# A mixer kernel on one core: the loads of w_v issued by GpSimd instead of SP

## The chip, the cores and the metric

The kernel runs on one core of a Trainium2 chip. The metric is the device time of one execution in microseconds (us); a row of times is the median of several executions. Besides the executions that are only timed, one is recorded by the hardware profiler, and all rows below are from that one.

## What is computed

Three stages follow each other; the batch is 4, the sequence 576 long, the model 512 wide with 8 heads of 64.

```python
# 1. causal attention with a bias from cumulative sums of s, 32 (batch, head) pairs
scores = scale * q @ k.T + min(-(cum_i - cum_j), 0);  attn = softmax(scores);  x = attn @ v
# 2. channel mix, d_ff = 1024
xk = mu_k * x + (1 - mu_k) * x_prev;  xr = mu_r * x + (1 - mu_r) * x_prev
k = relu(xk @ w_k);  v = (k * k) @ w_v;  r = sigmoid(xr @ w_r);  x = r * v
# 3. token mix (576 -> 256 -> 576) and channel mix (512 -> 1536 -> 512), both with a residual
u = x + token_mix(x);  out = u + relu(u @ w_ch1) @ w_ch2
```

The weights arrive with 8 bytes per element. So w_v, which is 1024 x 512, is 4 MB in memory, and each element has to be put together from two 32-bit words before TensorE can use it.

## The kernel before

The program is written as ordinary Python loops, and each piece of work carries a place in an order (`at(place)`). A planner then goes through all pieces, takes for each engine the one with the lowest place among those that are ready, and fixes one list per engine; the chip runs these five lists, each strictly in order, with semaphores between them. A DMA stands in the list of the engine that issues it. It holds that list for the time of its issue and, if what it writes into is still in use, until that is released. What stands behind it on that engine waits too.

The attention of batch 0 comes first. `early` (L301) does the first two blocks of 128 queries of its 8 heads, `late` (L350) the other three. They run scores on TensorE (L308, L358), a masked maximum on VectorE (L252), the exponential on ScalarE (L262), the sum's reciprocal on VectorE (L263, L264), the normalization of P on GpSimd (L265), transposes on TensorE (L316, L367), a copy on ScalarE and the product with v on TensorE (L326, L385). In the meantime the weights of stage 2 are prepared. Then come the attention of batches 1 to 3 (L277, L399, L447) and beside it the matmuls of stage 2: `up` with w_k (tile h), `gate` with w_r (tile r), `down` with w_v (tile vd), all at L109. Stage 3 ends the program, with nearly nothing but matmuls.

A weight is prepared piece by piece. `weight_load` (L538) takes a buffer and issues the load (L543) on the queue that its last argument names, SP if there is none. `weight_split` (L551) puts the two words together and splits the result into a high and a low part: two ScalarE instructions (L75, L555), two on VectorE (L556, L557), for w_v a halving on ScalarE, a copy of the high part on ScalarE (L75), and the subtraction that gives the low part (L561). That last one is on VectorE for w_v and on GpSimd for the other weights. It is also what releases the buffer. w_k and w_r come in 12 pieces of 512 KB, through five buffers of their own. w_v comes in 16 pieces of 256 KB. These pieces take their buffers from the pool `xt`, which has 6 and which also holds the attention's results `xt`, four of them for batch 0 from L329 on. That leaves two for the pieces of w_v. The weights of stage 3 (w_tok1, w_tok2, w_ch1, w_ch2) come much later, from the function `weight`, in 58 pieces of 128 to 288 KB; their loads are issued by GpSimd.

SP issues everything else: the loads of q, k and v, copies inside the chip (X<-HL, X<-ext_d), the stores.

The pieces of w_v have places from 18 on, in steps of 1.5; the first `late` item has place 16, the pieces of w_k and w_r have places 1.0 to 14.2.

```python
    x = 18
    for f in range(0, DM, 128):
        for k in range(0, KF, 2):
            with at(x):
                weight_load((k, f), rows(w_v, k, k + 2)[:, :, f:f + 128], S // 2, xt_p, "xt")
                weight_split((k, f), wv[:, 0, k:k + 2, f:f + 128], wv[:, 1, k:k + 2, f:f + 128], 1)
            x += 1.5
```

Of the kernel before, what the change touches and what calls it, by code (L numbers as in the profile page):

```python
# [24 lines left out]
def attention_moe_mixer(  # L25
# [16 lines left out]
    nc = tc.nc  # L42
    G, D, _, S = qk.shape
# [24 lines left out]
    def at(place):  # L68
        return tc.high_priority(tc.cur_priority - int(place * 1000))
# [13 lines left out]
    xt_p = ctx.enter_context(tc.tile_pool(name="xt", bufs=6))  # L83
# [60 lines left out]
    xt = {}  # L144
# [394 lines left out]
    def weight_load(key, sw, n, pool, tag, q=nc.sync):  # L539
        r, k, f = sw.shape  # L540
        t = pool.tile([128, n, 2], I32, tag=tag, name="raw")[:, 0:k * f].rearrange("p (k f) t -> p k f t", f=f)
        for r0 in range(0, 128, r):
            q.dma_start(out=t[r0:r0 + r], in_=sw.bitcast(I32).rearrange("p k (f t) -> p k f t", t=2))  # L543
        raw[key] = t
# [6 lines left out]
    def weight_split(key, hi, lo, half=0):  # L551
        t = raw.pop(key)
        low, high = t[:, :, :, 0], t[:, :, :, 1]
        copy("A", f32(high), f32(high), 2.0 ** -112)
        nc.scalar.activation(out=low.bitcast(U32), in_=low.bitcast(U32), func=AF.Copy, scale=TOP3, bias=-0.496)  # L555
        nc.vector.scalar_tensor_tensor(out=low, in0=high, scalar=3, in1=low, op0=ALU.logical_shift_left, op1=ALU.bitwise_or)  # L556
        nc.vector.scalar_tensor_tensor(out=low, in0=high, scalar=-2 ** 31, in1=low, op0=ALU.bitwise_and, op1=ALU.bitwise_or)  # L557
        if half:
            copy("A", f32(low), f32(low), 0.5)
        copy("A", hi, f32(low))  # L560
        (nc.vector if half else nc.gpsimd).tensor_tensor(out=lo, in0=f32(low), in1=f32(hi), op=ALU.subtract)  # L561

    def rows(sw, k0, k1):
        r0 = 128 * k0
        r = min(128, sw.shape[0] - r0)
        return sw[r0:r0 + r * (k1 - k0)].rearrange("(k p) f -> p k f", p=r)
# [119 lines left out]
    for y, a in enumerate(first):  # L686
        nm, W, sw, f = a
# [15 lines left out]
    for f in range(0, DM, 128):  # L703
        for k in range(0, KF, 2):
            with at(x):
                weight_load((k, f), rows(w_v, k, k + 2)[:, :, f:f + 128], S // 2, xt_p, "xt")
                weight_split((k, f), wv[:, 0, k:k + 2, f:f + 128], wv[:, 1, k:k + 2, f:f + 128], 1)
            x += 1.5
    with at(N0):
# [228 lines left out]
```

## Time and profile before

| | |
|---|---|
| median of 3 executions | 905.09 us (903.65 to 905.67) |
| profiled execution, its own time | 905.17 us |
| its span, first to last instruction | 903.4 us |
| TensorE matmul busy | 861.6 us (95%) |
| VectorE, ScalarE, GpSimd busy | 515.1, 464.8, 318.5 us |
| mean granted TensorE clock | 0.977 |

The profiled execution lies 0.08 us from the median, so its rows stand for the timed executions. 1.77 us of its time lie outside the span. PE is TensorE's matmuls, PEld its weight loads, DVE VectorE, ACT ScalarE, POOL GpSimd, SPq the DMA issues of SP. L543 is line 543 of the program. An arrow `<-` in brackets names what ended an idle time; `X<-HL` names a tile and what it is made from.

### The profile page before, as it was taken

To read this page: it belongs to the slowest core of one execution; us is meant where nothing else is said; L and a number is where in the kernel's file an instruction comes from. 1 tells how busy PE (TensorE), PEld (TensorE's weight loads), DVE (VectorE), ACT (ScalarE), POOL (GpSimd) and SP (SyncE) were. 2 spreads that over 40 slices of the span, in tenths; PEclk is the share of its full clock that TensorE was granted. 3 is DMA by queue.
4 is the path that set the end of the run, shared out by engine and by line. 5 is a ranking of instruction groups with operands and counts; after the bars stand their busy time and mean duration, and the time that the engine had idled before them with its cause. 6 is when DMAs were issued, how large, how long until landed. Compare 5 with 4: busy or idle time off the path is not lost.

```text
span 903.4 us, 16007 instructions
## 1 busy us (share of the span) xinstructions
PE 861.6 (95%) x5456; PEld 789.6 (87%) x5456; DVE 515.1 (57%) x1542; ACT 464.8 (51%) x1264; POOL 318.5 (35%) x463
## 2 busy tenths in 40 slices
PE   6679999999899999999999998999999999999998
PEld 4335678998789989989989998999999999999998
DVE  5687786777898587876657865871331212212120
ACT  4787876766786756758456774760320201112010
POOL 4555535644564535655144764550000000000000
PEclk9759999999999999999999999999999999999999
DMA  7973345456654336542032656564022020211100
GB/s 168 215 193 89 88 124 133 98 122 152 139 117 107 88 81 142 121 108 48 29 118 78 216 160 200 183 180 129 24 75 66 18 79 27 63 43 53 36 1 36
DMA packets 65089, 93.69 MB, mean 104 GB/s; under 512 B 7424, under 2 KB 45568, under 8 KB 65008
## 3 DMA queue, kind: packets, MB, share of 16 engines
q1 hardware_dynamic: 58560, 77.00, 33.1%
q0 software_dynamic: 4576, 15.08, 5.5%
q10 hardware_dynamic: 1872, 0.59, 0.3%
q8 instruction: 43, 0.70, 0.3%
q14 instruction: 38, 0.31, 0.1%
HBM read 56.11 MB, written 14.75 MB: 78 GB/s over the span
## 4 chain that ended last, share of the span: by engine, by line
PE 77%; DMA 8%; DVE 7%; ACT 3%; issue 2%; POOL 2%; SPq 0%; ACTq 0%; POOLq 0%; DVEq 0%
PE c L109 33%; PE vd L109 9%; PE h L109 9%; PE r L109 5%; PE t L109 5%; PE pv L447 4%; PE t L399 3%; PE s L358 3%; PE s L277 2%; PE pv L385 2%; PE s L278 2%; DMA X<-HL 2%; DMA raw<-in_moe_w_k_dram 1%; PE t L367 1%; DVE raw L556 1%
## 5 line engine op out<-in xcount | busy, mean ns | idle before, releaser
L784 ACT ACTIVATE HID<-c 128x384 fp32r<-128x384 f32 x72 | 35.4, 491 | 220.6 <-PE c L109 220.5
L265 POOL TENSOR_SCALAR P<-P,sum 64x576 f32<-64x576 f32 (+4 forms) x160 | 106.5, 670 | 113.9 <-DVE sum L264 58.5
L109 PE MATMUL h<-XK,WK 128*128 128x256 f32 (+1 forms) x768 | 122.9, 301 | 3.6 <-DVE XK L465 1.5
L109 PE MATMUL vd<-KK,WV 128*128 128x256 f32 (+1 forms) x768 | 119.3, 299 | 0.0
L109 PEld LDWEIGHTS h<-XK,WK 128*128 128x128 f32 x768 | 105.6, 188 | 7.9 <-DVE XK L465 2.1
L262 ACT ACTIVATE P<-P,mx 64x576 f32<-64x576 f32 (+4 forms) x160 | 95.8, 600 | 30.7 <-DVE mx L252 26.7
L109 PEld LDWEIGHTS vd<-KK,WV 128*128 128x128 f32 x768 | 105.8, 188 | 2.2 <-ACT raw L555 0.4
L109 PE MATMUL c<-HID,WV 128*128 128x384 f32 x576 | 104.9, 336 | 0.0
L109 PE MATMUL c<-U,WK 128*128 128x384 f32 x576 | 104.2, 337 | 0.5 <-DVE HID L785 0.5
L109 PEld LDWEIGHTS c<-U,WK 128*128 128x128 f32 x576 | 99.9, 188 | 1.1 <-DVE HID L785 0.8
L109 PEld LDWEIGHTS c<-HID,WV 128*128 128x128 f32 x576 | 100.7, 188 | 0.0
L252 DVE CUSTOM_DVE_ANT_0 P<-s,maskc 64x288 f32<-64x288 f32 (+4 forms) x160 | 75.0, 474 | 26.3 <-PE t L399 6.9
L785 DVE SCALAR_TENSOR_TENSOR HID<-c,HID 128x384 fp32r<-128x384 f32 x72 | 40.0, 556 | 87.0 <-ACT HID L784 86.9
L842 DVE TENSOR_TENSOR ut<-c,ut 128x384 f32<-128x384 f32 x24 | 13.4, 558 | 124.1 <-PE c L109 124.1
L477 POOL TENSOR_TENSOR KK<-k,KK 128x256 fp32r<-128x256 f32 (+1 forms) x64 | 54.1, 848 | 31.5 <-ACT k L476 31.2
L109 PE MATMUL r<-XR,WR 128*128 128x320 f32 (+1 forms) x384 | 60.0, 298 | 0.0
L556 DVE SCALAR_TENSOR_TENSOR raw<-raw 128x256 int32<-128x256 int32 (+2 forms) x85 | 47.1, 556 | 19.6 <-ACT raw L555 15.7
L75 ACT ACTIVATE raw<-raw 128x256 f32<-128x256 f32 (+2 forms) x101 | 46.9, 465 | 19.6 <-DMA raw<-in_moe_w_v_dram 6.6
L399 PE MATMUL t<-ident,P 128*128 128x128 f32 (+1 forms) x360 | 53.6, 262 | 2.1 <-DVE PT L425 1.6
L109 PE MATMUL c<-HID,WR 128*128 128x384 f32 x288 | 54.2, 336 | 0.0
L109 PEld LDWEIGHTS r<-XR,WR 128*128 128x128 f32 x384 | 53.0, 188 | 0.7
L109 PE MATMUL c<-U,C1A 128*128 128x384 f32 x288 | 52.9, 343 | 0.0
(111 smaller groups left out, 1627.6 us busy)
## 6 DMA issues: line engine op xcount, KB each, us to landing
X<-HL SPq DMA_DIRECT2D x72, 288.0 KB
raw<-in_moe_w_ch_dram POOLq DMA_DIRECT2D x48, 256.0 KB, 3.3
HL<-in_qk_dram SPq DMA_DIRECT2D x12, 576.0 KB
ut<-u_d SPq DMA_DIRECT2D x32, 192.0 KB
yt<-y_d SPq DMA_DIRECT2D x16, 288.0 KB
u_d<-yt SPq DMA_DIRECT2D x16, 288.0 KB
raw<-in_moe_w_k_dram SPq DMA_DIRECT2D x8, 512.0 KB
raw<-in_moe_w_v_dram SPq DMA_DIRECT2D x16, 256.0 KB
```

What stands on the lines that cost most here:

```text
L75: nc.scalar.activation(out=out, in_=in_, func=AF.Copy, scale=scale)
L109: nc.tensor.matmul(ps, a, b, start=first and i == 0, stop=last and i == n - 1)
L252: nc.vector.tensor_tensor_reduce(out=P[0:m, c0:c1], in0=ps[0:m, 0:c1 - c0], in1=maskc[0:m, 512 - q0 + c0:512 - q0 + c1], scale=-scale, sca ...
L262: nc.scalar.activation(out=P[0:m, 0:w], in_=P[0:m, 0:w], func=AF.Exp, bias=mx[0:m, x:x + 1], scale=-1.0, accum_out=sm[0:m, 0:1])
L265: nc.gpsimd.tensor_scalar(out=P[0:m, 0:w], in0=P[0:m, 0:w], scalar1=sm[0:m, 1:2], scalar2=1.0, op0=ALU.mult, op1=ALU.mult)
L358: nc.tensor.matmul(ps[0:m, 0:c1 - c0], x[0:D + 4, 0, q0:q0 + m], x[0:D + 4, 1, c0:c1], start=True, stop=True)
L399: nc.tensor.transpose(ps[0:r, p0 + m * k:p0 + m * k + m], P[0:m, 128 * k:128 * k + r], ident[0:m, 0:m])
L447: nc.tensor.matmul(ps[:, o:n], vv[0:r, k, :], pair[t], start=(k == 0 and t == 0), stop=(k == nk - 1 and t == 1),)
L477: nc.gpsimd.tensor_tensor(out=kk[:, 1, m, 0:n], in0=t[:, 0:n], in1=f32(kk[:, 0, m, 0:n]), op=ALU.subtract)
L556: nc.vector.scalar_tensor_tensor(out=low, in0=high, scalar=3, in1=low, op0=ALU.logical_shift_left, op1=ALU.bitwise_or)
L784: nc.scalar.activation(out=hi, in_=ps, func=AF.Relu)
L785: nc.vector.scalar_tensor_tensor(out=lo, in0=ps, scalar=0.0, in1=f32(hi), op0=ALU.max, op1=ALU.subtract)
```

## The change

The call that loads a piece of w_v is given a queue, GpSimd's. Pieces, sizes, buffers, places and the split stay as they are.

```diff
     for f in range(0, DM, 128):
         for k in range(0, KF, 2):
             with at(x):
-                weight_load((k, f), rows(w_v, k, k + 2)[:, :, f:f + 128], S // 2, xt_p, "xt")
+                weight_load((k, f), rows(w_v, k, k + 2)[:, :, f:f + 128], S // 2, xt_p, "xt", nc.gpsimd)
                 weight_split((k, f), wv[:, 0, k:k + 2, f:f + 128], wv[:, 1, k:k + 2, f:f + 128], 1)
             x += 1.5
```

## Rows read from the trace of the kernel before

**Rows 1.** The page's parts on the span and the engines' busy time.

```profile
span 903.4 us, 16007 instructions
PE 861.6 (95%) x5456; PEld 789.6 (87%) x5456; DVE 515.1 (57%) x1542; ACT 464.8 (51%) x1264; POOL 318.5 (35%) x463
```

**Rows 2.** Table by stretch: busy us of each engine, granted clock, DMA share, GB/s.

```profile
0.00:10.00 10.00, 3.24 (x10) 2.53 (x10) 4.88 (x22) 2.33 (x5) 3.67 (x21) 1.00 0.55 98
10.00:40.00 30.00, 21.44 (x70) 12.62 (x68) 18.84 (x78) 20.30 (x54) 14.72 (x26) 0.90 0.96 211
40.00:52.00 12.00, 11.30 (x21) 4.82 (x21) 7.43 (x20) 8.74 (x22) 7.74 (x9) 0.50 0.99 304
52.00:67.00 15.00, 10.23 (x29) 4.50 (x29) 14.60 (x37) 12.90 (x30) 7.26 (x5) 0.61 0.60 137
67.00:80.00 13.00, 11.07 (x57) 6.21 (x56) 8.83 (x27) 8.40 (x24) 8.14 (x8) 0.96 0.34 88
80.00:140.00 60.00, 60.00 (x386) 44.37 (x385) 45.42 (x148) 46.48 (x138) 26.23 (x36) 1.00 0.40 106
140.00:600.00 460.00, 444.53 (x3138) 416.28 (x3137) 342.96 (x1074) 318.19 (x893) 247.68 (x358) 0.99 0.47 122
```

**Rows 3.** Timelines around 63 to 73 us (start, duration): PE, POOL, then DVE.

```profile
72.39 0.51 PE L367 MATMUL t<-ident,P 64*128 64x64 f32 x5 [1.93 <-POOL P L265]
...
63.12 2.94 POOL L265 TENSOR_SCALAR P<-P,sum 128x384 f32<-128x384 f32 x1 [3.79 <-DVE sum L264]
...
88.18 0.59 POOL L265 TENSOR_SCALAR P<-P,sum 128x384 f32<-128x384 f32 x1 [1.08 <-ACT k L476]
...
62.85 0.40 DVE L556 SCALAR_TENSOR_TENSOR raw<-raw 128x256 int32<-128x256 int32 x1
...
64.61 0.41 DVE L557 SCALAR_TENSOR_TENSOR raw<-raw 128x256 int32<-128x256 int32 x1
...
65.61 1.32 DVE L557 SCALAR_TENSOR_TENSOR raw<-raw 128x256 int32<-128x256 int32 x2
```

**Rows 4.** Loads of w_v on SP: all 16 together, then two rows of SP's timeline.

```profile
L543 SPq DMA_DIRECT2D raw<-in_moe_w_v_dram x16: 367/370/1398, 38.6 to 123.9; - x16
...
38.62 1.64 SPq L543 DMA_DIRECT2D raw<-in_moe_w_v_dram  x2
...
70.33 0.37 SPq L543 DMA_DIRECT2D raw<-in_moe_w_v_dram  x1
```

**Rows 5.** Waits (us in total, times, longest): SP's and TensorE's weight loads'.

```profile
SPq L543 <- DVE WV L561: 20.3, 4, 13.6
...
PEld vd L109 <- DVE WV L561: 0.4, 1, 0.4
```

**Rows 6.** Line 543, 390 to 610 us: GpSimd's loads (ns min/median/max), their waits, their landing.

```profile
L543 POOL DMA_DIRECT2D raw<-in_moe_w_ch_dram x48: 536/546/633, 489.6 to 597.0; - x48
L543 POOL DMA_DIRECT2D raw<-in_moe_w_tok_dram x10: 530/550/732, 393.5 to 486.3; - x10
...
  DVE t L463: 3.4, 2
  DVE U L830: 2.8, 2
  DVE sum L263: 2.2, 1
...
DMA to landing us min/median/max: 2.4/3.3/5.5
```

**Rows 7.** Timelines of the opening: GpSimd's, then TensorE's first matmuls.

```profile
2.73 0.21 POOL L329 MEMSET xt<- 128x1 f32 x4
...
3.22 0.38 POOL masks.py:199 TENSOR_SCALAR_AFFINE_SELECT ident<-ident 128x128 f32<-128x128 f32 x1
9.35 0.95 POOL L185 MEMSET e<- 32x192 f32 x4 [5.76 <-DMA ext_d<-e]
...
6.76 1.62 PE L308 MATMUL s<-HL 66*128 66x128 f32 x4 [6.76 <-DMA HL<-in_qk_dram]
```

## The prediction

> **What bounds the kernel now.** I read the page's busy times first. TensorE's matmuls are busy for 861.6 of the 903.4 us of the span, GpSimd for 318.5 [rows 1]. So the first question is where TensorE is not busy. The table by stretch answers it [rows 2]. From 80 to 140 us TensorE is busy for all 60 us, and after that for 444.5 of 460 us until 600. The loose part is the opening: 3.2 of the first 10 us, 21.4 of the next 30, 10.2 of the 15 us from 52 on, 11.1 of the 13 from 67 on. Whatever brings the start of the full stretch forward is worth its whole length at the end, since the matmuls behind it are the same; whatever happens beside the full stretch is worth nothing unless TensorE comes to wait for it.
>
> In the opening the limit changes. [...] From 52 to 67 us VectorE is full, 14.6 of 15 us [rows 2]. Then GpSimd is last: at 72.39 us TensorE's transposes had waited 1.93 us for a normalization of P on GpSimd, and the one that began at 63.12 us took 2.94 us where the same shape took 0.59 us at 88.18 us [rows 3].
>
> The loads of w_v stand in this picture as follows. SP issues 16 of them, the first two at 38.62 us, the last at 123.9 us [rows 4]. Two buffers carry all 16, so from the third on a load waits for the subtraction L561 of the piece two before it. SP's list was held up by that for 20.3 us in 4 waits, once for 13.6 us, which ends with the load at 70.33 us [rows 4, 5]. TensorE has no large wait from these pieces: its weight loads for vd waited 0.4 us for w_v's last step [rows 5].
>
> **The change, part by part.** *Removed from SP:* 16 issues of 0.37 us (the median; the longest is 1.40 us), 5.9 us of issuing, and the 20.3 us of waits that stood in front of SP's later loads and stores [rows 4, 5]. I cost the gain at nothing. In the full stretch TensorE waits for none of SP's transfers, and the load that was held for 13.6 us had behind it only loads for later heads. If that cover is gone, SP's transfers are at most earlier.
>
> *Added to GpSimd:* 16 issues. The 58 loads that GpSimd issues later in the program show the price: 0.53 to 0.73 us each, median 0.55 us, so 8.7 us in all [rows 6]. In the full stretch of 60 us GpSimd is busy for 26.2 us, so the 33.8 us of idle time take in some 12 of them, 6.6 us, at no cost. From 67 to 80 us GpSimd is on the path. There two loads fall now (one at 70.33 us [rows 4], the next close behind). On the path both would cost 1.1 us, behind the normalizations none. I take one, +0.55 us.
>
> *Added waits:* a load in GpSimd's list waits there for its buffer, and behind it stand the normalizations of P (TensorE's transposes wait for them) and the subtractions for w_r. Of the 58 later loads, 5 waited for VectorE, 8.4 us in all, 1.7 us each [rows 6]. The planner puts a load behind what it takes to be done by the time of the release, so I take 0 here and put the wait among the rivals.
>
> *Moved in time:* GpSimd has nothing to do from 3.6 us, where the last step for the identity ends, until 9.35 us. The four memsets of `xt` at 2.73 us, which belong to heads 1, 3, 5 and 7, show that its list takes whatever is ready, out of the program's order [rows 7]. At that time the two spare buffers are free. So I expect the first two loads of w_v in this gap and not at 38.62 us. That has two consequences. The first is on the DMA engines. 0.52 MB leave the stretch from 40 to 52 us, where 304 GB/s were moved at a share of 0.99: a gain of up to 1.7 us. They come into the first 10 us, where the share is 0.55, so some 4.5 us of the engines' time are free; at the 211 GB/s of the next stretch the two loads want 2.5 us [rows 2]. They fit, but they share the engines with the first loads of q and k, for which TensorE waits until 6.76 us [rows 7]; that could cost up to 2.5 us. I take half of the gain, -0.8 us, as TensorE at half clock is a limit of that stretch as well.
>
> The second consequence is on VectorE. With the first pieces split early, the third and fourth get their buffers early as well. Their four instructions (first at 62.85, last within 65.61 us, three of 0.4 us and a part of 1.32 us, some 1.9 us) leave the stretch in which VectorE is full and in which GpSimd's 2.94 us normalization lies [rows 2, 3]. That normalization is 2.35 us over its price elsewhere, which bounds the gain; the other bound is 0, if the fifth and sixth piece take the same place. I take the four instructions' own time, -1.9 us.
>
> [...]
>
> *At the end of w_v:* pieces that run one round ahead take away the 0.4 us that vd's weight loads waited [rows 5], -0.4 us.
>
> **The sum.** +0.55 - 0.8 - 1.9 - 0.4 = -2.55 us, against the profiled execution's 905.17 us (span 903.4 and 1.77 around it): 902.6 us. That execution lies 0.08 us from the median of the runs, so no correction is made. With all gains at their bounds and no issue on the path it is -2.35 - 1.7 - 0.4 = -4.45 us, 900.7 us.
>
> **The rivals.** *No change.* What bounds the opening is work that the change doesn't touch (VectorE's instructions on w_k and w_r, the attention), and the fifth and sixth pieces take the place of the third and fourth; the full stretch hides the rest. For it speaks that TensorE waits for w_v only 0.4 us [rows 5]. Then all terms but small ones are 0, and the time is 905.2 us. [...]
>
> *GpSimd held by a load.* Slower: a load in the stretch from 67 to 80 us reaches the head of GpSimd's list before its buffer is free, and a normalization of P that TensorE is waiting for stands behind it. It decides from the point where the subtraction that releases the buffer comes later on VectorE than the planner took it to. For it: one such wait on SP lasted 13.6 us [rows 5], and GpSimd is the last releaser just there [rows 3]. Against it: 53 of 58 later loads did not wait [rows 6]. Two loads at 0.55 + 1.7 us are +4.5 us with no gain: 909.7 us.
>
> *The early loads crowd the opening.* The 2.5 us bound above falls on the path of q and k and of the first piece of w_k, and no gain follows: 907.7 us. For it speaks that the DMA engines are full from 10 us on [rows 2], against it the idle 4.5 us before.
>
> *Late landing.* The loads from GpSimd land in 5.5 us, the longest of the later ones, not in 3.3 us, the median [rows 6]. Through two buffers that adds 2.2 us in each of 7 rounds, 15.4 us for the last piece; less a lead of about a round (some 11 us: the loads run from 38.6 to 123.9 us in 8 rounds) it is some +4 us: 909 us. [...]
>
> **How the numbers follow.** The forecast has a chance of 0.40, no change 0.27, GpSimd held 0.18, the crowded opening 0.11, late landing 0.04. About 0.2%, 1.8 us, is what a measurement of this kernel can tell from no change. So faster is 0.40, the same 0.27, slower 0.33. The range runs over the rivals on the slow side to 909.7 us; on the other side it starts at 900.7 us. The planner lays all five lists anew, and TensorE idles for 15.5 us between 140 and 600 us [rows 2], which a new order can move either way. I add a sixth of that, some 2.5 us, at each end: 898 to 912 us.
>
> **What would show it.** Right: two loads of w_v on GpSimd before 10 us; the second pair well before 48 us; no 2.9 us normalization near 63 us; the full stretch of TensorE beginning 2 to 3 us earlier than about 72.4 us, with the same busy time behind it. Wrong: the first loads still near 38 us (then no change), an idle time of GpSimd in front of L543 of over 1 us followed by TensorE's transposes waiting (held), TensorE's first matmul clearly after 6.76 us (crowded). A different order of stage 2 between 140 and 600 us, with TensorE's idle time moved by several us there, would make the prediction wrong for a reason that no row of before shows.

## The result, and the profile after

The changed kernel takes 909.94 us, median of 7 runs (906.87 to 912.39), beside 905.09 us for the kernel before in the same rounds: ratio 1.0053, 95% interval 1.0033 to 1.0073. It is slower by about 4.8 us, where 2.5 us less were forecast. The profiled execution took 911.34 us, 6.2 more than that of before. Some of the shortened kernels below ran in two groups of executions 1 to 3% apart; where a median has a second one beside it, that one is of the faster group.

The page of the kernel after, its parts on the span and on TensorE's busy time (beside [rows 1]):

```profile
span 909.4 us, 16008 instructions
PE 867.7 (95%) x5456; PEld 793.1 (87%) x5456; DVE 520.9 (57%) x1542; ACT 461.3 (51%) x1264; POOL 325.9 (36%) x479
```

The 16 loads are there (479 instructions on GpSimd for 463). The table by stretch of the kernel after, with the columns of [rows 2]:

```profile
0.00:10.00 10.00, 1.81 (x6) 1.67 (x7) 4.47 (x16) 2.66 (x6) 5.54 (x23) 1.00 0.70 150
10.00:40.00 30.00, 23.82 (x67) 13.62 (x65) 22.52 (x93) 25.85 (x73) 19.10 (x29) 1.00 1.06 278
40.00:52.00 12.00, 11.37 (x24) 4.87 (x25) 10.05 (x24) 7.67 (x17) 7.84 (x11) 1.00 0.91 238
52.00:67.00 15.00, 9.11 (x25) 4.27 (x24) 14.97 (x30) 10.91 (x27) 6.63 (x7) 1.00 0.25 75
67.00:80.00 13.00, 12.86 (x54) 6.88 (x54) 8.68 (x32) 8.55 (x25) 8.14 (x9) 1.00 0.24 68
80.00:140.00 60.00, 59.62 (x377) 43.10 (x378) 45.02 (x140) 41.89 (x122) 27.53 (x41) 1.00 0.37 98
140.00:600.00 460.00, 443.25 (x3119) 414.46 (x3118) 338.69 (x1064) 312.48 (x885) 244.40 (x354) 0.99 0.47 120
```

Three things are to be seen. The DMA engines now work in the first 40 us (278 GB/s for 211) and have little to do from 52 us on. From 52 to 67 us VectorE is full still, 14.97 of 15 us, but with 30 instructions where it did 37. And TensorE got less far: 25 matmuls from 52 to 67 us for 29, 54 from 67 to 80 us for 57, and 377 from 80 to 140 us for 386. Busy time alone would have said the contrary for 67 to 80 us.

The 1.00 in the clock column up to 67 us must not be read as full speed. The trace of the kernel after has no reading of the clock before 73.3 us (that of before none before 27 us), and the column then shows 1.00. Matmuls of one shape tell more. In the kernel before, two products `s` of 68x288 at a reading of 1.00, two of 68x512 at 0.50, and the clock there (TensorE's busy time, matmuls, clock, DMA share, GB/s):

```profile
54.48 0.70 PE L358 MATMUL s<-X 68*64 68x288 f32 x2
61.70 2.07 PE L358 MATMUL s<-X 68*128 68x512 f32 x2 [2.90 <-DVE mx L252]
54.50:57.50 3.00, 1.14 (x5) 1.00 1.04 191
60.00:65.00 5.00, 3.30 (x5) 0.50 0.13 41
```

and in the kernel after:

```profile
66.02 2.08 PE L358 MATMUL s<-X 68*128 68x512 f32 x2 [0.73 <-DVE mx L252]
```

The two of 68x288 take 1.22 us there (at 60.80 us, below). By these times TensorE at 61 and 66 us after still ran as it does at a reading of 0.50, as it mostly did from 34 to 68 us before (0.50 from 34 to 52 us, 0.61 in the mean from 52 to 67 us).

GpSimd's loads of w_v in the kernel after (ns min/median/max, idle time before them, who waited, landing), beside [rows 4 to 6]:

```profile
L543 POOL DMA_DIRECT2D raw<-in_moe_w_v_dram x16: 722/758/879, 2.9 to 114.1; - x16
its engine sat idle before it (us, times) until:
  DVE WV L561: 12.4, 7
  DVE sum L263: 6.8, 2
  DVE t L462: 0.6, 1
who waited for it (us, times):
  ACT raw L75: 11.0, 7
...
DMA to landing us min/median/max: 3.0/4.0/7.5
```

An issue takes 0.76 us, not 0.55; ten of the 16 had to wait, 19.8 us in all. And their places, from GpSimd's timeline of the kernel after (the first six):

```profile
2.89 1.62 POOL L543 DMA_DIRECT2D raw<-in_moe_w_v_dram  x2
...
13.29 0.74 POOL L543 DMA_DIRECT2D raw<-in_moe_w_v_dram  x1 [2.80 <-DVE sum L263]
...
16.13 0.76 POOL L543 DMA_DIRECT2D raw<-in_moe_w_v_dram  x1
...
27.30 0.76 POOL L543 DMA_DIRECT2D raw<-in_moe_w_v_dram  x1 [4.94 <-DVE WV L561]
...
39.12 0.76 POOL L543 DMA_DIRECT2D raw<-in_moe_w_v_dram  x1
```

When the kernel before issues its first, the kernel after issues its sixth. That pulls the split of w_v forward, into the time in which w_k and w_r are split and the attention starts. The work on the tile `raw` (all pieces of w_k, w_r and w_v) by stretch, after and then before (columns: VectorE, ScalarE, GpSimd with instructions, clock, DMA share, GB/s):

```profile
0.00:40.00 40.00, 13.59 (x24) 17.39 (x36) 11.64 (x11) 1.00 0.97 246
40.00:67.00 27.00, 18.64 (x18) 13.72 (x27) 7.55 (x6) 1.00 0.54 147
```

```profile
0.00:40.00 40.00, 9.59 (x12) 10.95 (x18) 6.02 (x4) 0.92 0.86 183
40.00:67.00 27.00, 13.65 (x22) 15.44 (x32) 6.16 (x5) 0.56 0.77 211
```

VectorE has done 42 such instructions by 67 us, in 32.2 us; in before 34, in 23.2 us. That is 9 us more of the engine that limits the stretch, for eight more instructions. One row explains nearly half of it. VectorE's timeline of the kernel after:

```profile
55.22 0.40 DVE L556 SCALAR_TENSOR_TENSOR raw<-raw 128x256 int32<-128x256 int32 x1
55.65 4.62 DVE L557 SCALAR_TENSOR_TENSOR raw<-raw 128x256 int32<-128x256 int32 x1
60.19 0.55 DVE L252 CUSTOM_DVE_ANT_0 P<-s,maskc 128x384 f32<-128x384 f32 x1
60.66 0.08 DVE L252 DVE_READ_ACCUMULATOR2_ANT mx<- 128x1 f32 x1
```

and GpSimd's at the same time:

```profile
50.72 0.76 POOL L543 DMA_DIRECT2D raw<-in_moe_w_v_dram  x1 [0.57 <-DVE WV L561]
51.53 0.72 POOL L265 TENSOR_SCALAR P<-P,sum 128x512 f32<-128x512 f32 x1
52.23 1.73 POOL L561 TENSOR_TENSOR WK<-raw,WK 128x512 fp32r<-128x512 f32 x1
55.47 0.76 POOL L265 TENSOR_SCALAR P<-P,sum 64x576 f32<-64x576 f32 x1 [1.51 <-DVE sum L264]
56.20 1.29 POOL L561 TENSOR_TENSOR WK<-raw,WK 128x512 fp32r<-128x512 f32 x1
57.46 2.52 POOL L561 TENSOR_TENSOR WR<-raw,WR 128x512 fp32r<-128x512 f32 x2
```

The bitwise operation of 0.41 us [rows 3] took 4.62 us. It began as GpSimd was in the first of four instructions that follow each other without a gap, and ended 0.3 us after the last. The same instruction takes 4.62 us in e6, a further run with all loads on GpSimd. Behind it stands the step on P of shape 128x384 that TensorE waits for: TensorE's next product `s` had waited 3.65 us, as its timeline in the kernel after shows:

```profile
60.80 1.22 PE L358 MATMUL s<-X 68*64 68x288 f32 x2 [3.65 <-DVE mx L252]
```

GpSimd's four took 0.76, 1.29 and, two together, 2.52 us, and VectorE's instruction did not end between any two of them. What in the hardware holds it these rows do not show.

To see where the lag arises I compare at equal matrix work: the matmuls are summed in order, each with the median distance from one of its shape to the next in the trace of before, and the times are compared at which the same sum is reached. In us later than before, at the time of before in the first line (the rows e1, e3 and e16 are runs told of below):

```
                          20    57    88   195   246   289   374   end
after                    2.0   6.1   1.8   1.3   1.8   3.9   6.1   6.0
e1  first two           -1.0   2.4   0.8   0.8   4.7   5.4   4.9   7.0
e16 3rd to 8th on SP    -1.0  -2.1  -3.4  -3.4   0.7   5.3   4.2   4.2
e3  SP, other order     -1.9  -0.6  -0.6  -0.2   1.3   1.1   2.0  -0.5
```

After is 6 us behind at 57 us and makes up for most of it, since TensorE is not full before 80 us; 1.8 us stay at 88 us. The rest of the 6.0 us comes later: the lag is 3.9 us at 289 us, some 2 us again at 364 us, and 6.1 us at 374 us, far behind the last piece of w_v. There TensorE's timeline of the kernel after has

```profile
372.21 1.57 PE L447 MATMUL pv<-PT,VV 128*128 128x320 f32 x8 [1.82 <-DVE xt L454]
```

and its table the stretch

```profile
370.00:377.00 7.00, 5.18 (x28) 4.73 (x26) 6.72 (x25) 6.31 (x21) 6.38 (x9) 0.76 0.65 129
```

with 28 matmuls in 7 us, at a mean clock of 0.76 behind a gap; the same stretch in the kernel before has 58 at full clock:

```profile
370.00:377.00 7.00, 7.00 (x58) 6.53 (x57) 5.87 (x21) 6.93 (x22) 7.00 (x11) 1.00 0.57 129
```

There are two questions, then: what the loads cost in the opening, and what a new order of the instructions costs behind it.

### The profile page after: what moved, and what is told of

Same layout as the page of the kernel before. It is cut to its first block, busy times and chain, and to the rows that moved or that the text cites. A ratio compares the mean times of both kernels' runs of the same rounds, so it can differ in the third digit from the quotient of the medians.

```text
span 909.4 us, 16008 instructions
## 1 busy us (share of the span) xinstructions
PE 867.7 (95%) x5456; PEld 793.1 (87%) x5456; DVE 520.9 (57%) x1542; ACT 461.3 (51%) x1264; POOL 325.9 (36%) x479
## 4 chain that ended last, share of the span: by engine, by line
PE 71%; DMA 10%; DVE 9%; issue 5%; ACT 3%; POOL 2%; SPq 1%; POOLq 0%; ACTq 0%; DVEq 0%
PE c L109 32%; PE vd L109 8%; PE h L109 7%; PE r L109 5%; PE t L109 4%; PE pv L447 3%; PE t L399 3%; DMA X<-HL 3%; PE s L277 2%; DMA HL<-in_qk_dram 2%; PE s L278 2%; PE pv L385 1%; DVE raw L556 1%; DMA raw<-in_moe_w_k_dram 1%; DVE P L252 1%
## 5 line engine op out<-in xcount | busy, mean ns | idle before, releaser
L265 POOL TENSOR_SCALAR P<-P,sum 64x576 f32<-64x576 f32 (+4 forms) x160 | 101.6, 640 | 114.9 <-DVE sum L264 45.1
L109 PE MATMUL h<-XK,WK 128*128 128x256 f32 (+1 forms) x768 | 125.0, 304 | 1.9 <-ACT k L474 1.1
L109 PEld LDWEIGHTS h<-XK,WK 128*128 128x128 f32 x768 | 108.5, 192 | 5.3 <-ACT k L474 1.5
L556 DVE SCALAR_TENSOR_TENSOR raw<-raw 128x256 int32<-128x256 int32 (+2 forms) x85 | 44.9, 529 | 24.1 <-ACT raw L555 20.5
L557 DVE SCALAR_TENSOR_TENSOR raw<-raw 128x256 int32<-128x256 int32 (+2 forms) x85 | 57.3, 678 | 1.1
```

Of the source, the lines that this page charges most:

```text
L109: nc.tensor.matmul(ps, a, b, start=first and i == 0, stop=last and i == n - 1)
L265: nc.gpsimd.tensor_scalar(out=P[0:m, 0:w], in0=P[0:m, 0:w], scalar1=sm[0:m, 1:2], scalar2=1.0, op0=ALU.mult, op1=ALU.mult)
```

## The experiments

**Parts of the change in the whole kernel.** The loads are divided between the two issuers:

```diff
-weight_load((k, f), ..., S // 2, xt_p, "xt", nc.gpsimd)
+weight_load((k, f), ..., S // 2, xt_p, "xt", nc.gpsimd if f == 0 and k < 4 else nc.sync)   # e1: first two
+weight_load((k, f), ..., S // 2, xt_p, "xt", nc.sync if f == 0 and k < 4 else nc.gpsimd)   # e2: last 14
```

> Only the first two pieces of w_v are loaded from GpSimd, the other 14 from SP as before. Theory A (the pieces now come too early: the first two loads at 3 us share the DMA engines with q and k, and their successors bring VectorE work into 40 to 67 us): TensorE's full stretch begins about 2 us late as in the changed kernel, and the time is 1 to 3 us over before, apart from what a new order later does. Theory B (GpSimd's list is held by issues and waits of the 16 loads): 14 of the 16 holds are gone, the opening is as before within 0.5 us. Theory C (the planner's new order of stage 2 and of batches 1 to 3 makes the difference): the time can be anywhere within 4 us of before, and the lag at the start of stage 3 isn't the one at 85 us.

Measured 910.49 us (904.78 to 913.22), ratio 1.0040 [1.0010, 1.0070].

> The first two pieces of w_v stay on SP and so are loaded near 38 us, the other 14 are loaded from GpSimd. Theory A: no load of w_v before 38 us, so the opening is as before within 0.5 us, and the time too, apart from a new order later. Theory B: 14 issues of 0.76 us and their waits for buffers stay in GpSimd's list; TensorE is 1 to 2 us late by 135 us. Theory C: anywhere within 4 us of before, decided after 200 us.

Measured 916.31 us (914.64 to 923.03), ratio 1.0137 [1.0070, 1.0204]. Each part alone is as bad as the whole or worse, so the time is no sum of the parts. By the table at equal work, e1 is 0.8 us behind at 195 us and 4.7 at 246 us. Whatever costs it most lies where w_v has long been loaded. It doesn't strike each time: of e1's ten executions three took 904.8 to 905.6 us, as long as before, and seven 910.2 to 913.2.

**Another order behind the opening, with the loads left where they are.** The units of stage 2 get another place in the planner's order; the lists are the same up to about 120 us and are planned anew behind it:

```diff
-            with at(N0 + n + 3):
+            with at(N0 + n + 3.3):   # e3 (loads on SP), e4 (on GpSimd); 2.7 for e11 (SP), e12 (GpSimd)
```

> The kernel before with one number changed that has nothing to do with loads: the units of stage 2 get a place 0.3 later. The lists of all engines stay the same up to about 120 us and are planned anew after it. Theory C: the time moves by 2 to 6 us from before in either direction. Theories A and B: by under 1.5 us.

> The changed kernel with the same number changed as in the run before it (the units of stage 2 a place 0.3 later). Theory C: the difference to its partner with SP is not 5 us but the 1 to 2.5 us that the opening has, or even has the other sign, as the orders after 120 us are new for both. Theories A and B: again some 5 us slower than its partner.

> The whole kernel before with the units of stage 2 a place 0.3 earlier: the same opening, another order behind 120 us than that of before and than the one with places 0.3 later. Theory C (a new order by itself costs some us, because that of before happens to be a good one): 3 to 6 us over before. Otherwise within 1.5 us of it, as with the places 0.3 later (0.7 us over).

> The whole changed kernel with the units of stage 2 a place 0.3 earlier. If the cost is the opening's 3.1 us alone, 3 us over its partner with SP; if the loads on GpSimd cost something behind the opening as well, 5 to 9 us, as in the two pairs so far (4.9 and 8.9 us).

Measured, beside the two kernels themselves:

```
place      loads on SP              loads on GpSimd          distance
+3         905.09                   909.94                    4.8
+3.3  e3   906.83 (904.70-912.03)   e4  915.70 (910.63-918.66)  8.9
+2.7  e11  916.13 (908.20-918.72)   e12 913.27 (909.23-915.30) -2.9
```

The same loads with another order behind them differ by up to 11 us on SP (905.1 to 916.1) and 5.8 on GpSimd. The distance of the pairs is 3.6 us in the mean, with both signs, though the negative one is not sure: e11's five executions alone span 908 to 919 us. A single pair of whole kernels therefore can't tell what the loads cost. The part up to where the lists are the same can. At equal work, at 88 us, the three openings with the loads on GpSimd (after, e4, e12) are 1.8, 2.7 and 1.7 us behind before, and the two others with SP (e3, e11) 0.6 and 2.9 us ahead of it. So executions of the same opening differ by up to 2.9 us, and the two kinds by 3.2 us in the mean, without overlap.

**The opening by itself.** Batches 1 to 3, the second half of stage 2 of batch 0 and stage 3 are left out; the results so far are stored. What remains has the lists of the whole kernels up to 95 to 125 us:

```diff
-    for n in range(NI):
+    for n in range(N1):
         attention_item(n)
...
+            nc.sync.dma_start(out=out[0, 128 * p:128 * p + 128, :], in_=xt[0, p][:, 1:1 + S])
```

> The kernel before, cut: it leaves out batches 1 to 3 of the attention, the second half of batch 0 of stage 2 and all of stage 3, and stores the attention's result of batch 0. The lists are those of before up to about 125 us. It is the yardstick for the three runs beside it; about 145 to 155 us.

> The changed kernel, cut in the same way, so that the opening is measured by itself and nothing that is planned anew behind it counts. If the loss sits in the opening (theories A and B), it is 2 to 4 us slower than its yardstick with SP; if it comes from the new order behind it (theory C), within 0.7 us of it.

> The same cut with only the first two loads of w_v on GpSimd, the other 14 on SP. Theory A (too early): as slow as with all 16, 2 to 4 us over the yardstick. Theory B (GpSimd's list held): within 0.7 us of the yardstick.

> The same cut with the first two loads on SP and the last 14 on GpSimd. Theory A: within 0.7 us of the yardstick. Theory B: 2 to 4 us over it.

Two more divide the loads at the eighth (`nc.gpsimd if f < 256 else nc.sync`, and the reverse):

> The cut of before's opening again (batches 1 to 3, the second half of batch 0 of stage 2 and stage 3 left out), with the first 8 loads of w_v on GpSimd and the last 8 on SP. The yardstick with SP took 147.6 us, all 16 on GpSimd 150.7, the first two alone 145.4. If the cost comes from loads 3 to 8, which hold GpSimd's list before TensorE's full stretch, 150 to 151 us; if it comes from the loads in the full stretch from 80 us on, 145 to 146 us.

> The same cut with the first 8 loads on SP and the last 8, all of them in or just ahead of TensorE's full stretch, on GpSimd. If the full stretch hides GpSimd's issues and waits, 147.6 us within 0.7; if they count there too, 149 us or more.

Measured, and the distance to e5 (all executions, then the faster group):

```
e5   all on SP                  147.61 (146.52-150.38)          147.09
e6   all on GpSimd              150.69 (150.08-153.19)   +3.1   150.62   +3.5
e7   first two on GpSimd        145.42 (144.69-147.06)   -2.2   145.42   -1.7
e8   last 14 on GpSimd          149.57 (148.97-150.57)   +2.0   149.57   +2.5
e9   first eight on GpSimd      153.75 (152.27-155.75)   +6.1   152.59   +5.5
e10  last eight on GpSimd       147.69 (146.84-151.50)   +0.1   147.65   +0.6
```

Here the change costs 3.1 us, or 3.5. The first two loads gain some 2 us, and the last eight, which fall beside the full stretch, cost 0.1 to 0.6. What costs comes with the third to eighth: e9 less e7 is 8.3 us (7.2 in the faster group), e8 less e10 is 1.9 us. The size depends on the company, the sign doesn't.

Not all of this is time that GpSimd or VectorE takes. From 70 to 80 us, where TensorE's first matmuls with w_k fall, its rows in e5, e8 and e10 are (columns as above):

```profile
70.00:80.00 10.00, 8.31 (x47) 1.00 0.55 144
70.00:80.00 10.00, 9.92 (x30) 0.66 0.33 85
70.00:80.00 10.00, 10.00 (x24) 0.51 0.31 87
```

At equal work e8 was 2.4 us ahead of before at 65 us and 1.5 behind at 80 us; e10 went from 2.7 ahead to 3.6 behind, and e5 stayed 0.7 ahead. The lists of e5 and e10 are the same up to 92 us, and the profiled execution of e10 is its longest, 151.50 us, where the other four took 146.84 to 147.79. So executions of the same lists that differ in the clock lie 4.3 us apart at 80 us, and e8 was no later than e5 until its clock fell. How far the distances in the table come by way of the clock was not taken apart.

**Is GpSimd's bunch the cause?** Without w_r's low half two of the four instructions beside the 4.62 us are gone, while VectorE's list stays the same to beyond the step on P:

```diff
-        (nc.vector if half else nc.gpsimd).tensor_tensor(out=lo, in0=f32(low), in1=f32(hi), op=ALU.subtract)
+        lo is None or (nc.vector if half else nc.gpsimd).tensor_tensor(out=lo, in0=f32(low), in1=f32(hi), op=ALU.subtract)
...
-weight_split((nm, f), W[:, 0, :, f:f + 128], W[:, 1, :, f:f + 128])
+weight_split((nm, f), W[:, 0, :, f:f + 128], W[:, 1, :, f:f + 128] if W is wk else None)
```

> All 16 loads of w_v on GpSimd, shortened opening, and GpSimd's four subtractions that make the low half of w_r left out (the product with w_r reads the high half twice instead), so that two of the four GpSimd instructions that ran back to back at 55.5 to 60.0 us are gone (WR x2, 2.52 us). The lists of VectorE are the same to the normalization multiply behind it. Theory H (the loads hold GpSimd, its instructions bunch up behind, and VectorE's bitwise operation on `raw` 128x256 is held for the whole bunch, 4.62 us against 0.41): that instruction falls to about 2.0 us, `P` 128x384 on VectorE comes at about 57.7 us instead of 60.4, and the time lies 2 to 3 us under the 150.7 of the same opening with the subtractions. Theory V (it is w_v's split work that stands earlier in VectorE's and ScalarE's lists, whatever GpSimd does): the time falls by no more than that of the opening with SP's loads when it loses the same four instructions, and the pair stays 3 us apart.

> The control: loads on SP, shortened opening, the same four subtractions left out and the high half read twice. Both theories: 147.6 less 0 to 1 us, since in that opening no VectorE instruction is held longer than about 1.8 us.

VectorE's timeline of e13:

```profile
54.77 2.13 DVE L557 SCALAR_TENSOR_TENSOR raw<-raw 128x256 int32<-128x256 int32 x1
56.82 0.55 DVE L252 CUSTOM_DVE_ANT_0 P<-s,maskc 128x384 f32<-128x384 f32 x1
```

and GpSimd's of e13:

```profile
54.59 0.77 POOL L265 TENSOR_SCALAR P<-P,sum 64x576 f32<-64x576 f32 x1 [1.51 <-DVE sum L264]
55.33 1.29 POOL L561 TENSOR_TENSOR WK<-raw,WK 128x512 fp32r<-128x512 f32 x1
```

The instruction falls from 4.62 to 2.13 us and again ends 0.3 us behind GpSimd's last, as theory H has it, and the whole falls by 2.6 us to 148.07 (147.91 to 148.74). That the bunch holds VectorE is thus shown. But the control e14 fell by 5.2 us, to 142.44 (140.15 to 144.01; faster group 140.67), where 0 to 1 was expected, so the distance of the pair grew to 5.6 us. By the totals that is what theory V was to give. The lists of each are those of its original up to about 65 us, so equal work compares them where before stands at 57 us: there GpSimd's opening lies 6.7 us behind SP's with the subtractions and 2.7 us without. So the bunch makes some 4.0 of 6.7 us at that point, as far as single traces can tell: two of the same lists lie up to 2.9 us apart. The rest is something else: in VectorE's timeline of e14 the same step on P stands at

```profile
52.44 0.55 DVE L252 CUSTOM_DVE_ANT_0 P<-s,maskc 128x384 f32<-128x384 f32 x1
```

4.4 us before e13's, of which the held instruction explains 1.7 (2.13 less 0.41). In VectorE's list 16 of the second bitwise operations stand ahead of that step with the loads on GpSimd, nine with SP. What the new lists behind 65 us contribute to e14's end was not taken apart.

**Does it add up, and is there a better division?** Loads 3 to 8 go back to SP, the others stay on GpSimd, in the opening (e15) and in the whole kernel (e16):

```diff
+weight_load((k, f), ..., S // 2, xt_p, "xt", nc.sync if (f == 0 and k >= 4) or f == 128 else nc.gpsimd)
```

> Shortened opening, loads 1 and 2 and the last eight on GpSimd, loads 3 to 8 on SP. If the costs of the groups add up (first two -2.2, last eight 0.1 against 147.6): 145.5 us. If the last eight cost nothing only because SP's own queue was late already: 147 or more.

> The same division of the loads in the whole kernel. By the opening alone: 2.1 us under before, ratio 0.998. The plan behind the opening is another one, and plans alone moved this kernel by up to 10 us either way, so 903 to 913; the lag counted at equal matrix work at 135 us tells what the opening gave: about -2 us there.

e15 measured 145.97 us (144.17 to 147.33; faster group 144.93): 1.6 us under SP's opening and 4.7 under GpSimd's, the latter by the six loads alone. e16 measured 909.39 us (905.08 to 914.55), ratio 1.0039 [1.0020, 1.0058]. Its opening is 3.4 us ahead of before, and stays so up to 195 us (table above); then it loses 4.1 us by 246 us and 4.6 us by 289 us. At the first place TensorE's timeline of e16 has

```profile
232.96 1.34 PE L447 MATMUL pv<-PT,VV 128*128 128x320 f32 x8 [1.97 <-DVE xt L454]
```

and behind this gap the table by stretch of e16

```profile
235.00:245.00 10.00, 9.21 (x41) 7.96 (x41) 9.41 (x30) 7.43 (x21) 7.18 (x10) 0.51 0.78 162
```

where that of the kernel before is

```profile
235.00:245.00 10.00, 7.93 (x59) 6.84 (x59) 9.91 (x29) 7.90 (x24) 7.43 (x11) 1.00 0.90 180
```

A gap of 2 us, then half the clock for some 10 us, at which TensorE is "busy" for 9.2 us and does 41 matmuls in place of 59. Such a gap isn't always followed by this: behind the one of 1.93 us that ends at 72.39 us in before [rows 3] the clock reads 1.00 up to 225 us. No version of the whole kernel here beats the kernel before.

**GpSimd held, or w_v's work too early?** All loads on ScalarE leave GpSimd as free as SP does, with w_v's work about as early in VectorE's list as with GpSimd; eight buffers on GpSimd make GpSimd wait less and the work earlier still:

```diff
+weight_load((k, f), ..., S // 2, xt_p, "xt", nc.scalar)                      # e17
-    xt_p = ctx.enter_context(tc.tile_pool(name="xt", bufs=6))
+    xt_p = ctx.enter_context(tc.tile_pool(name="xt", bufs=8))                # e18
```

> All 16 loads of w_v issued by ScalarE, shortened opening. GpSimd's list is as free as with SP, and w_v's split work stands about as early in VectorE's list as with GpSimd's loads: 14 of the second bitwise operations and five finished pieces stand ahead of the second `P` 128x384 (16 and five with GpSimd, 9 and two with SP). Theory H (what costs is GpSimd's held list): 144 to 147 us, near the opening with the first two alone on GpSimd (145.4), plus what waiting costs ScalarE. Theory V (what costs is w_v's work standing earlier): 149 to 151, near the opening with all on GpSimd (150.7).

> All 16 loads of w_v on GpSimd, shortened opening, and eight buffers instead of six in the pool of w_v's pieces, so that GpSimd waits less for a buffer, and w_v's work stands earlier still: 20 of the second bitwise operations and six pieces ahead of the second `P` 128x384. Theory H (GpSimd's list held by its waits and issues): faster than the 150.7 with six buffers, 148 or less. Theory V (work standing earlier): slower, 152 or more.

e17 measured 150.25 us (148.04 to 150.35; faster group 148.62), e18 162.86 us (160.49 to 165.52; faster group 161.13). By the totals of all executions both go with theory V; by its faster group e17 lies between the two. The traces don't bear theory V out. At equal work e17 is 1.4 us behind before at 57 us, where e6 is 6.1 us behind and e5 0.7 us ahead: with GpSimd free, most of what lies between e6 and e5 is gone at that point. From 44 to 58 us no bitwise operation takes over 1.12 us, and w_r's first subtraction on GpSimd stands at 61.81 us, behind the stretch. It gets to 3.3 us behind by 80 us, at a clock of

```profile
70.00:80.00 10.00, 8.53 (x32) 0.66 0.28 84
```

How early the work stands doesn't decide by itself either. Ahead of the second step on P of 128x384 VectorE's list has 9 of the second bitwise operations with SP (e5), 13 in e7, 14 in e17, 16 in e6; the step begins at 52.3, 50.8, 55.8 and 60.4 us. e7 has done as many instructions on `raw` by 67 us as the kernel after, 42, and gains. e18 decides nothing: at equal work it is 11.7 us behind at 30 us already, so that its loss arises ahead of the stretch at 55 us: its first 10 us have 207 GB/s, a DMA share of 0.80 and four matmuls, where those of e6 have 165, 0.73 and seven. And in e17 ScalarE takes both the issues (0.37 us each) and 4.1 us of waiting for landings, so that the 2.1 us to e5 that remain at 57 us need not be the early work.

## Why the prediction was wrong

- **What bounds the opening.** Right. TensorE waits there, VectorE is full from 52 to 67 us before and after (14.60 and 14.97 of 15 us), and what is done beside the full stretch is nearly free: the last eight loads on GpSimd cost 0.1 to 0.6 us (e10). Three of the signs came true (two loads before 10 us, the second pair at 13 and 16 us, no normalization of 2.9 us near 63 us), and the 1.93 us that TensorE waited for GpSimd are gone. In their place it waits 3.65 us for VectorE at 60.80 us.
- **The first two loads in GpSimd's gap.** They came there, at 2.89 us, and by themselves gain nearly what was forecast: -2.2 us (e7; -1.7 in the faster group) where the terms for DMA, VectorE and the end of w_v sum to -3.1. Whether by those terms isn't shown. TensorE's first matmul went from 6.76 to 8.19 us, the mark of the crowded opening, but e7 has the same two loads and gains, so that rival didn't decide.
- **"Four instructions leave VectorE's full stretch", -1.9 us.** This is the step that failed, by its sign. They left, and more than their number took the place: the planner did not stop at the third and fourth piece but went on with the fifth to seventh at 27 to 51 us. The bound that I had set at 0 ("the fifth and sixth piece take the same place") was no bound. A list that takes whatever is ready takes w_v's work ahead of w_r's and of the attention's, and VectorE had 9 us more of `raw` by 67 us, not 1.9 us less. The count of instructions is not what costs, since e7 has the same 42 by then, in 28.4 us for 32.2; what differs is that in after one of them met GpSimd's bunch. That the four instructions made the normalization of 2.94 us long was an estimate from the two standing side by side in [rows 3]; no run shows it.
- **SP's freed queue, at nothing.** The text said "at most earlier", as if earlier could not cost. Without the pair of w_v loads at 38.62 us, w_r's first load went from 44.88 to 40.08 us, and its first low half on GpSimd from 66.02 to 57.46 us. That put w_r's subtractions into the bunch that held VectorE for 4.62 us. Early work on w_r alone doesn't do it: in e7 its first low half begins at 53.65 us, but there the step on P, at 50.77 us, is ahead of it. Of the 6.7 us that the shortened opening lies behind at 57 us, w_r's subtractions make some 4.0 (e13, e14).
- **Issues and waits on GpSimd.** The issue was put at 0.55 us with one on the path; it is 0.76 us, 12.1 us for 16. The waits were put at 0: ten loads waited, 19.8 us, of which I had taken "53 of 58 later loads did not wait" as evidence from a stretch that has other buffers and other neighbours. The rival "held by a load" (909.7 us) names about the right time, and it is right that normalizations and subtractions stand behind the load, but its place and mechanism are wrong. It had TensorE wait for GpSimd at 67 to 80 us. In the trace VectorE is what TensorE waits for, at 57 to 61 us, and VectorE is what GpSimd's instructions hold; the load isn't among them. "Late landing" didn't decide: the loads landed in 4.0 us in the median, 7.5 at the longest, but the last was issued at 114.1 us, not 123.9.
- **The order behind it.** The text gave 2.5 us at each end for it and named it as what no row of before shows. The runs put it at up to 11 us on SP alone (e3, e11). Of after's 6.0 us at the end, 4.2 arise behind 88 us.

What stays open is the share of the held VectorE, of early work and of TensorE's clock in the 3.1 us of the opening, since the parts don't add up (+2.0, +0.1, -2.2 and +6.1 against +3.1) and the clock differs between executions; and whether the order behind it is worse with GpSimd's loads for a reason or by chance: three pairs give +4.8, +8.9 and -2.9 us.

## What to carry to other kernels

Where a planner takes whatever is ready, moving loads to a free queue moves the work that they release, and that work competes on the engine that limits the stretch (here 9 us more of VectorE by 67 us): look at what the earlier data sets going and which instructions of another engine it meets, not only at what the issue costs. Earlier is not free for transfers either, since it decides which instructions of two engines meet (here w_r's first load came 4.8 us earlier, and one of VectorE's took 4.62 us for 0.41). Before a gain or loss of half a per cent is put down to an edit, run the same edit with another order behind it, and cut the program where the lists begin to differ. And before two clocks are compared, see that matmuls of one shape bear the column out (here two of 68x288 took 0.70 us at a reading of 1.00 in before, and 1.22 us where the column of after shows 1.00 without a reading).

## What the hardware showed

- A VectorE instruction on `raw` was held through a run of GpSimd instructions without a gap, not through one: 4.62 us through four (after and e6), 2.13 us through two (e13). It took 0.41 us with GpSimd idle (after, at 65.19 us), and as much in before at 64.61 us, within the normalization that took 2.94 us [rows 3].
- A load of w_v takes GpSimd 0.72 to 0.88 us, a later load of w_ch of the same 256 KB from the same line 0.55 us in the median [rows 6]. A piece of w_v has two rows of 1 KB per partition and one of w_ch one of 2 KB; whether that or the stretch makes the difference wasn't tried. A load of w_v took SP and ScalarE 0.37 us in the median.
- A gap of 1.97 us on TensorE was followed by a clock of 0.51 over 10 us (e16 at 235 us), one of 1.82 us by 0.76 over 7 us (after at 370 us); one of 1.93 us at 72 us in before was not. From 70 to 80 us, where matmuls stand close, there were 30 and 32 of them at 0.66 (e8, e17) for 47 at 1.00 (e5). Ahead of that, where TensorE waits in part (busy for 27.7 of the 37 us from 30 to 67 us in e5), a cost of the lower clock could not be seen: e5, at 0.50 from 20 to 67 us, is 0.7 us ahead at 57 us of before, which read 1.00 from 54 to 58 us.
